# A linear-attention and GELU-MLP kernel: paired inverses on opposite corners, masked copies, casting and transposing DMAs

## Chip, cores and metric

The kernel runs on one core of a Trainium2 chip. The metric is the device time of one execution in microseconds. Lower is better.

## What is computed

The inputs are `q`, `k`, `v` (4 batches x 8 heads x 768 tokens x 48, float32), `beta` (4 x 8 x 768) and two MLP weights (384 x 2048 and 2048 x 384). First comes attention with a delta rule, token by token, and then an MLP over each token's 8 x 48 = 384 outputs:

```python
k_n = k / (np.linalg.norm(k, axis=-1, keepdims=True) + 1e-06)
for t in range(S):
    y[:, :, t] = einsum('bhd,bhde->bhe', q[:, :, t], state)
    v_old = einsum('bhde,bhd->bhe', state, k_n[:, :, t])
    state = state + beta[t] * einsum('bhd,bhe->bhde', k_n[:, :, t], v[:, :, t] - v_old)
...
out = gelu_tanh(x @ w_in) @ w_out
```

## The kernel before

**Chunks and units.** The 768 tokens are cut into 12 chunks of 64. The 32 pairs of batch and head are cut in two sets of 16. One chunk of one set is a *unit*: 24 units `u`, chunk `c = u // 2`. Within a unit, 16 small problems lie as 8 groups `g` by two partition halves `a` (partitions 0 to 63 and 64 to 127).

**One unit.** `prep(u)` normalizes `k` (POOL squares it, DVE sums, POOL takes the square root at L486, DVE adds and inverts), makes `kn`, `kb` (times beta) and `qb`, transposes them on TensorE (L506, 48 matmuls of 64x64) and copies the result to `kT` on DVE (L508). Two gram products follow (L529, L523); DVE multiplies them by masks into `mnd` (L532, L536), and POOL adds or subtracts an identity to make `lt` and `at` (L540, L542). The inverse of a 64x64 unit triangular matrix is then found by five Newton rounds (L558): `left` (L548) multiplies `lt` and `at` into a PSUM bank, DVE adds twice the identity and writes `qf`, `q4` or `q5` (L565), `right` (L553) multiplies that by `lt`, and ACT or DVE copies the result back to `lt` (L408 through L569). Each step needs the one before it.

`chain(u)` carries the state over chunks: `carried` (L589) and a subtraction (L605), `queries` (L594), `values` with the inverse (L599), the new state (L616, L622), the output `omat` (L627), and its copy to `xo`. When both units of a chunk are done, six DMAs on SP (L637) move 16 rows each of the fourth part of `xo` into the gaps of the other three, so that 384 features lie on 3 x 128 partitions.

**The MLP.** `mlp_up(c)` runs 16 blocks of `W1` (L651) with a GELU on ACT (L655); `mlp(u)` multiplies by `W2` (L668), copies to `ob` and stores. `weights()` loads both weights in float32 by DMAs on SP into two staging buffers `wst` (L452), and ACT and DVE cast them to bf16 (L408 through L457).

**Where matmuls lie in the array.** A small matmul uses one quarter of the array: input half by output half. Groups whose input and output halves are the same are mode `d` (diagonal), those that cross are mode `o`. Two groups, one of each mode, are issued interleaved by twos (`together`, L273) when the planner pairs them. The MLP, mode `m`, uses the whole array.

**The order.** Every operation is added to a list with its engines, a duration, a key and the buffers it reads and writes. `Flow.schedule` (L79) plays the list through, always taking the ready operation with the lowest key on each engine, and the order in which it places them becomes each engine's program. Where an operation names several engines, the planner chooses one. For TensorE it counts matmuls in blocks of 128 (`BLOCK`) and lets a block begin no sooner than 3.6 us after the last (`REFILL`). Key `2 * c + 4.5` places a chunk's MLP behind the units of some two chunks to come. `emit` turns dependencies into semaphore waits. Each engine then runs its list in order, and so does each DMA queue's issuer, SP, ACT or POOL.

Before the loop, DVE clears PSUM (L678) and POOL writes constant columns of `q4`, `q5`, `kn`, `kb` and `qb` (L681, L684).

Of the kernel before, what the change touches and what calls it, by code (L numbers as in the profile page):

```python
# [7 lines left out]
F32 = mybir.dt.float32  # L8
BF16 = mybir.dt.bfloat16
ALU = mybir.AluOpType  # L10
# [3 lines left out]
C = 64  # L14
# [9 lines left out]
class Flow:  # L24
# [6 lines left out]
    GROUP = {"d": 64, "o": 64, "x": 64}  # L31
    OTHER = {"d": "o", "o": "d"}
    SLACK = 0.6
    DMA_LAT = 2.2
    BLOCK = 128
    REFILL = 3.6
# [9 lines left out]
    def add(self, eng, fn, dur, reads=(), writes=(), key=0.0, alloc=(), accum=(), frees=(), mode=None, dma=None, n=16):  # L46
# [30 lines left out]
        return o  # L77

    def schedule(self):  # L79
# [78 lines left out]
        while done < len(self.ops):  # L158
            for e in ENGINES:
                while free[e] <= t + 1e-9:  # L160
# [6 lines left out]
                    if o.dma is not None:  # L167
                        dma_free = max(dma_free, t + 0.65) + d
                        free[e], o.t1 = t + 0.65, dma_free + self.DMA_LAT
                        self.queues[e].append(o)  # L170
                        heapq.heappush(events, (o.t1, o.seq, o))
                    elif e == "pe":
# [12 lines left out]
                        for k in range(first, many + 1, self.BLOCK):  # L185
                            at = start + extra + long * k / many
                            hold = max(0.0, self.begun + self.REFILL - at)
                            extra += hold
                            self.begun = at + hold
# [130 lines left out]
def bass_deltanet__then__act_gelu_tanh_kernel(  # L320
# [19 lines left out]
    with nc.allow_non_contiguous_dma("strided loads"), nc.allow_low_precision("bf16 pipeline"):  # L340
# [5 lines left out]
        NR, NP, NX = 3, 5, 3  # L346
        ident = sb("ident", [128, 128], F32)
        id64 = sb("id64", [128, C])
        two64 = sb("two64", [128, C])
        mfull = sb("mfull", [128, 2, 128], F32)  # L350
        mneg = sb("mneg", [128, C], F32)
        mup = sb("mup", [128, 2, C], F32)
        half = sb("half", [128, G], F32)
        braw = sb("braw", [32, NC, 2, C], F32)
        bsb = sb("bsb", [128, NC, 2 * G], F32)
# [3 lines left out]
        kn, kb, qb = (sb(n, [128, G, C], BF16, NP) for n in ("kn", "kb", "qb"))  # L359
        vb = sb("vb", [128, G, D], BF16, NP)  # L360
        kT = sb("kT", [128, 3, G, C], BF16, NP)
        mnd = sb("mnd", [128, 3, G, C], BF16, NP)
        at, lt, qf, q4, q5 = (sb(x, [128, G, C], BF16, NP) for x in ("at", "lt", "qf", "q4", "q5"))
        vd = sb("vd", [128, G, D], BF16, 3)
        us = sb("us", [128, G, D], BF16, 3)
        st = sb("st", [128, G, D], BF16, 4)
        xo = sb("xo", [128, J, 2, 128], BF16, NX)
        gT = sb("gT", [128, FC, 256], BF16, 2)
# [3 lines left out]
        wst = sb("wst", [128, FF], F32, 2)  # L372
# [5 lines left out]
        PEO, T1, T2 = 0.01, 0.0165, 0.029  # L378
        KUP, KSTEP, KDN = 4.5, 0.08, 0.6


        def const():
# [6 lines left out]
            for x, cm in ((0, 1), (1, -1)):  # L389
                A("pool", lambda e, P, x=x, cm=cm: e.affine_select(  # L390
                    out=mfull[:, x, :], in_=mfull[:, x, :], compare_op=ALU.is_gt, fill=0.0, base=0,
                    pattern=[[-cm, 128]], channel_multiplier=cm), 0.4, reads=["mfull"], writes=["mfull"])
            for a in range(2):
# [5 lines left out]
                A("dve", lambda e, P, r=r: e.tensor_copy(mneg[r, :], mfull[r, 0, r]), 0.25, reads=["mfull"], writes=[f"mneg{a}"])  # L399
                A("dve", lambda e, P, r=r: e.tensor_copy(mup[r, 0, :], mfull[r, 1, r]), 0.25, reads=["mfull"], writes=[f"mupa{a}"])  # L400
                A("dve", lambda e, P, r=r: e.tensor_scalar(mup[r, 1, :], mfull[r, 1, r], -1.0, None, op0=ALU.mult), 0.2,
                  reads=["mfull"], writes=[f"mupb{a}"])

        ID, TWO = ["id640", "id641"], ["two0", "two1"]
        MNEG, MUP = ["mneg0", "mneg1"], ["mupa0", "mupa1", "mupb0", "mupb1"]
# [7 lines left out]
        EV = ("act", "dve")  # L413

        def load_beta():
# [9 lines left out]
            for a in range(2):  # L425
                r = half_rows(a)
                A("dve", lambda e, P, a=a, r=r: e.tensor_copy(
                    bsb[r, :, :], P("psb")[r, 0:32 * NC].rearrange("p (c g a) -> p c g a", a=2, g=2 * G)[:, :, :, a]), 0.4,
                  writes=[f"bsb{a}"], frees=["psb"], key=-10)
        BS = ["bsb0", "bsb1"]  # L430

        def load(c):
            s = c % NR
            for n, src in (("k", k), ("q", q), ("v", v)):
                view = src.rearrange("b (j a) (c t) d -> a c t (b j) d", a=2, t=C)
                for bp in range(2) if c == 0 else (None,):
                    gs = slice(0, 2 * G) if bp is None else slice(G * bp, G * bp + G)
                    for a in range(2):
                        A(("sp", "act") if c == 0 else "sp", lambda e, P, n=n, a=a, view=view, gs=gs: e.dma_start(  # L439
                            raw[n][s][half_rows(a), gs, :], view[a, c, :, gs, :]),  # L440
                          1.2 if bp is None else 0.6, writes=[f"{n}raw{s}{x}" for x in ((0, 1) if bp is None else (bp,))],
                          dma=f"d{n}{s}" if bp is None else f"e{n}{bp}", key=2 * c - 4.0 + (bp or 0) - (2 if c < 2 else 0))

        def weights():
            wi = moe_w_in.rearrange("(h d) f -> h d f", d=D)
            idx = [0]

            def stage(parts, dst, cols, key, wname):
                i = idx[0] % 2
                idx[0] += 1  # L450
                for rows, src in parts:
                    A("sp", lambda e, P, i=i, rows=rows, src=src: e.dma_start(  # L452
                        wst[i][rows, 0:cols] if len(src.shape) == 2 else
                        wst[i][rows, 0:cols].rearrange("p (n e) -> p n e", e=DM), src),
                      4.5 / len(parts), writes=[f"wst{i}"], dma=f"w{i}", key=key)
                for c0 in range(0, cols, 512):
                    A(("act", "dve"), lambda e, P, i=i, c0=c0: copy(e, dst[:, c0:c0 + 512], wst[i][:, c0:c0 + 512]),  # L457
                      {"act": 0.62, "dve": 0.6}, reads=[f"wst{i}"], writes=[f"{wname}_{c0}"], key=key + 0.5)

            for t in range(3):  # L460
                parts = [(slice(0, 48), wi[2 * t]), (slice(48, 64), wi[6, 16 * t:16 * t + 16, :]),
                         (slice(64, 112), wi[2 * t + 1]), (slice(112, 128), wi[7, 16 * t:16 * t + 16, :])]
                stage(parts, W1[:, t, :], FF, -1.5 + 0.1 * t, f"W1{t}")
            w2v = moe_w_out.rearrange("(n p) e -> p n e", p=128)
            w2f = W2[:, :, :].rearrange("p n e -> p (n e)")
            for i in range(0, FC, 4):
                stage([(slice(0, 128), w2v[:, i:i + 4, :])], w2f[:, i * DM:(i + 4) * DM], 4 * DM, -1.2 + 0.02 * i, f"W2{i}")

        def prep(u):
# [9 lines left out]
            bcol = bsb[:, c, G * bp:G * bp + G].unsqueeze(2).to_broadcast(full)  # L479
            POOL = ("pool", "dve") if u < 2 else "pool"  # L480
            tt = {"pool": 0.84, "dve": 0.55}
            A(POOL, lambda e, P: e.tensor_tensor(sqs[:, :, :], kr, kr, ALU.mult), tt,  # L482
              reads=[f"kraw{r}"], writes=[sqn], key=u)
            A("dve", lambda e, P: e.tensor_reduce(nr[:, 0, :], sqs[:, :, :], AX.X, ALU.add), 0.55,  # L484
              reads=[sqn], writes=[n("nrm")], key=u)
            A("pool", lambda e, P: e.tensor_tensor(nr[:, 1, :], nr[:, 0, :], half[:, :], ALU.pow), 1.65,  # L486
              reads=[n("nrm"), "half"], writes=[n("nrm")], key=u)
            A("dve", lambda e, P: e.tensor_scalar(nr[:, 2, :], nr[:, 1, :], 1e-6, None, op0=ALU.add), 0.38,
              reads=[n("nrm")], writes=[n("nrm")], key=u)
            A("dve", lambda e, P: e.reciprocal(nr[:, 3, :], nr[:, 2, :]), 0.2, reads=[n("nrm")], writes=[n("nrm")], key=u)  # L490
            A(POOL, lambda e, P: e.tensor_tensor(kn[s][:, :, 0:D], kr,  # L491
                                                   nr[:, 3, :].unsqueeze(2).to_broadcast(full), ALU.mult), tt,
              reads=[f"kraw{r}", n("nrm")], writes=[n("kn")], key=u)
            A(POOL, lambda e, P: e.tensor_tensor(kb[s][:, :, 0:D], kn[s][:, :, 0:D], bcol, ALU.mult), tt,
              reads=[n("kn"), *BS], writes=[n("kb")], key=u)
            A(POOL, lambda e, P: e.tensor_copy(qb[s][:, :, 0:D], qr), {"pool": 0.5, "dve": 0.4}, reads=[f"qraw{r}"], writes=[n("qb")],
              key=u + 0.01)
# [228 lines left out]
```

## Time and profile before

| | |
|---|---|
| runs, us | 345.94, 345.88, 344.78 (median 345.88) |
| profiled execution, us | 342.66, its span 340.9 |
| busy: PE, DVE, ACT, POOL | 280.3, 216.6, 141.2, 186.1 us |
| matmuls | 8556, of which 960 are the MLP's |
| DMA | 27.04 MB in 84284 packets, 77552 of them under 512 B |
| MLP matmuls busy, L651 and L668 | 78.6 and 75.8 us |
| mean of one: L486, L540, L542 on POOL | 1651, 1162, 1153 ns |
| mean of one: L508, L532, L536 on DVE | 953, 684, 1217 ns |

PE is TensorE's matmuls, PEld its weight loads, SP the engine that issues most DMAs. The span runs from the first to the last instruction; the execution's time has a little more around it. In a view of instruction groups each line has the source line, the engine, the operation and the tiles (output, then inputs), the shapes and the count. "issue" as the cause of a wait means that the engine waited for nothing that the profile shows. Matmuls are pipelined, so that their busy times overlap and a busy PE is not one at its peak. The share of DMA is the mean over 16 DMA engines; in a stretch it can stand a little over 1.

### The profile page before, as it was taken

The numbers are of one execution on the slowest core, as the hardware profiler recorded it, in microseconds if no ns is written. First come the engines' busy times: TensorE is split into PE (matmuls) and PEld (weight loads), VectorE is DVE, ScalarE is ACT, GpSimd is POOL, SyncE is SP. The second block draws the span as 40 slices with busy tenths as digits, with TensorE's granted clock in tenths as the row PEclk, the third lists the DMA queues.
The fourth block names the chain that finished last, engine by engine and source line by source line (L and its number), as shares of the span: only waits on it lengthen the run. The fifth ranks groups of instructions, "written<-read, shape, count | busy, mean of one in ns | idle before, by whom it ended". The sixth has DMA issues, their size and how long they took to land.

```text
span 340.9 us, 18321 instructions
## 1 busy us (share of the span) xinstructions
PE 280.3 (82%) x8556; PEld 210.8 (62%) x8556; DVE 216.6 (64%) x383; ACT 141.2 (41%) x258; POOL 186.1 (55%) x222
## 2 busy tenths in 40 slices
PE   1354773596989997997998898899898999999994
PEld 1353763485766665775765667576666667676772
DVE  7686583575849887757876777767675485751100
ACT  1014212253455432553345444444455545455462
POOL 8995786288678988748637866735416132000000
PEclk9999999999999999999999999999999999999999
DMA  8999999869793256036025040020020010111121
GB/s 134 174 166 157 162 170 190 124 156 183 151 160 71 55 116 124 9 78 118 7 50 95 12 96 4 10 53 11 4 50 10 15 40 8 29 31 25 30 50 46
DMA packets 84284, 27.04 MB, mean 79 GB/s; under 512 B 77552, under 2 KB 83824, under 8 KB 83824
## 3 DMA queue, kind: packets, MB, share of 16 engines
q1 hardware_dynamic: 80512, 25.18, 41.4%
q8 instruction: 67, 1.10, 1.5%
q10 hardware_dynamic: 3696, 0.69, 1.4%
q14 instruction: 9, 0.07, 0.1%
HBM read 20.55 MB, written 4.72 MB: 74 GB/s over the span
## 4 chain that ended last, share of the span: by engine, by line
PE 74%; issue 9%; DVE 5%; SPq 5%; DMA 4%; ACT 2%
PE ps L651 21%; PE ps L668 20%; PE ps L553 9%; PE ps L548 8%; PE ps L506 5%; DMA wst<-in_moe_w_in_dram 4%; SPq L439 3%; PE ps L523 2%; PE ps L599 2%; PE ps L627 2%; PE ps L529 1%; PE ps L589 1%; SPq L452 1%; PE ps L594 1%; PE ps L616 1%
## 5 line engine op out<-in xcount | busy, mean ns | idle before, releaser
L655 ACT ACTIVATE gT<-ps 128x512 bf16<-128x512 f32 x96 | 57.3, 597 | 68.2 <-PE ps L651 67.2
L651 PE MATMUL ps<-xo,W 128*128 128x256 bf16 x576 | 78.6, 277 | 2.4 <-issue 1.8
L408 ACT ACTIVATE lt<-ps 128x512 bf16<-128x512 f32 (+2 forms) x88 | 46.6, 535 | 76.7 <-PE ps L553 68.9
L668 PE MATMUL ps<-W,gT 128*128 128x384 bf16 x384 | 75.8, 328 | 1.1 <-issue 1.0
L651 PEld LDWEIGHTS ps<-xo,W 128*128 128x128 bf16 x576 | 51.6, 99 | 14.3 <-issue 2.0
L548 PE MATMUL ps<-at,lt 64*64 64x64 bf16 (+2 forms) x1536 | 44.7, 198 | 3.7 <-DVE lt L408 1.2
L548 PEld LDWEIGHTS ps<-at,lt 64*64 64x64 bf16 x1536 | 35.6, 118 | 16.4 <-issue 8.5
L668 PEld LDWEIGHTS ps<-W,gT 128*128 128x128 bf16 x384 | 33.0, 98 | 18.9 <-issue 0.9
L553 PE MATMUL ps<-lt,qf 64*64 64x64 bf16 x1152 | 35.1, 204 | 11.0 <-issue 9.2
L542 POOL TENSOR_TENSOR at<-mnd,id 128x512 bf16<-128x512 bf16 x24 | 27.7, 1153 | 28.1 <-DVE mnd L532 27.0
L486 POOL TENSOR_TENSOR nrm<-nrm,half 128x8 f32<-128x8 f32 x24 | 39.6, 1651 | 4.9 <-DVE nrm L484 4.9
L565 DVE TENSOR_TENSOR qf<-ps,two 128x512 bf16<-128x512 f32 x48 | 32.7, 684 | 11.7 <-PE ps L589 6.5
L540 POOL TENSOR_TENSOR lt<-mnd,id 128x512 bf16<-128x512 bf16 x24 | 27.9, 1162 | 21.0 <-DVE mnd L536 19.9
L565 DVE TENSOR_TENSOR q<-ps,two 128x384 bf16<-128x384 f32 (+1 forms) x48 | 23.3, 487 | 24.8 <-PE ps L548 19.5
L553 PEld LDWEIGHTS ps<-lt,qf 64*64 64x64 bf16 x1152 | 27.2, 118 | 17.3 <-issue 10.8
L491 POOL TENSOR_TENSOR kn<-kraw,nrm 128x384 bf16<-128x384 f32 x24 | 19.9, 828 | 24.6 <-PE ps L627 16.7
L408 DVE CAST lt<-ps 128x512 bf16<-128x512 f32 (+2 forms) x32 | 19.2, 601 | 20.1 <-PE ps L553 13.8
L536 DVE TENSOR_TENSOR mnd<-ps,mup 128x1024 bf16<-128x1024 f32 x24 | 29.2, 1217 | 2.5 <-PE ps L523 2.3
L508 DVE COPY kT<-ps 112x1536 bf16<-112x1536 bf16 x24 | 22.8, 953 | 7.8 <-PE ps L506 7.3
L553 PE MATMUL ps<-lt,q 64*64 64x48 bf16 (+1 forms) x768 | 23.1, 193 | 5.3 <-issue 2.6
L553 PEld LDWEIGHTS ps<-lt,q 64*64 64x64 bf16 x768 | 17.8, 117 | 13.4 <-issue 6.9
L482 POOL TENSOR_TENSOR sq<-kraw 128x384 f32<-128x384 f32 x23 | 19.0, 827 | 5.4 <-DMA kraw<-in_k_dram 5.4
(72 smaller groups left out, 447.1 us busy)
## 6 DMA issues: line engine op xcount, KB each, us to landing
out_dram<-ob SPq DMA_DIRECT2D x48, 96.0 KB, 2.2
kraw<-in_k_dram SPq DMA_DIRECT2D x22, 192.0 KB, 5.2
qraw<-in_q_dram SPq DMA_DIRECT2D x22, 192.0 KB, 4.7
vraw<-in_v_dram SPq DMA_DIRECT2D x22, 192.0 KB, 5.5
wst<-in_moe_w_out_dram SPq DMA_DIRECT2D x4, 768.0 KB, 7.7
wst<-in_moe_w_in_dram SPq DMA_DIRECT2D x6, 384.0 KB, 7.5
xo<-xo SPq DMA_DIRECT2D x72, 8.0 KB, 2.2
wst<-in_moe_w_in_dram SPq DMA_DIRECT2D x6, 128.0 KB, 8.2
```

The source lines that it names most:

```text
L408: return e.activation(out, in_, ACT.Copy) if e is nc.scalar else e.tensor_copy(out, in_)
L486: A("pool", lambda e, P: e.tensor_tensor(nr[:, 1, :], nr[:, 0, :], half[:, :], ALU.pow), 1.65, reads=[n("nrm"), "half"], writes=[n("nrm")] ...
L508: A("dve", lambda e, P: e.tensor_copy(kT[s][0:DP, :, :, :].rearrange("p x g t -> p (x g t)"), P(ps("T")).bitcast(BF16)[0:DP, 0:3 * 512]), ...
L536: A("dve", lambda e, P: e.tensor_tensor(z0[:, 1:3, :, :].rearrange("p x g t -> p g x t"), P(ps("G")).rearrange("p (g x t) -> p g x t", x=2 ...
L540: A("pool", lambda e, P: e.tensor_tensor(lt[s][:, :, :], z0[:, 1, :, :], eye, ALU.add), 1.16, reads=[n("z0n")] + ID, writes=[n("lt")], key=u)
L542: A("pool", lambda e, P: e.tensor_tensor(at[s][:, :, :], z0[:, 0, :, :], eye, ALU.subtract), 1.16, reads=[n("z0m")] + ID, writes=[n("at")] ...
L548: yield e.matmul(cols(P, name, 0, g, w)[r, :], x[r, g, :], y[r, g, 0:w])
L553: yield e.matmul(cols(P, name, 0, g, C - lo, lo)[r, :], q[r, g, :], lt[s][r, g, lo:C])
L565: A("dve", lambda e, P, q=q, pq=pq, w=w, add=add: e.tensor_tensor(q[:, :, 0:w], g1(P, pq, 0, w), add[:, :, 0:w], ALU.add), 0.15 + 0.00104 ...
L651: yield e.matmul(P(ph)[:, 256 * f:256 * f + 256], W1[:, t, 128 * (i + f):128 * (i + f) + 128], xo[xi][:, t, :, :].rearrange("p b t -> p (b ...
L655: A("act", lambda e, P, i=i, ph=ph: e.activation(gT[gi][:, i:i + 2, :].rearrange("p f t -> p (f t)"), P(ph), ACT.Gelu_apprx_tanh), 0.62, f ...
L668: yield e.matmul(P(po)[:, 0:DM], g_[:, f, 128 * bp:128 * bp + 128], W2[:, f, :], start=(f == 0), stop=(f == FC - 1))
```

## The change

The planner gets a mode `z`, a longer `DMA_LAT` (2.6), 4.0 for weights, 1.5 us for a DMA issue on POOL and `SLOWFILL`: 5.5 us per block of 128 matmuls before 45 us. A chunk's MLP key falls to `2.5 + 0.75 * c` for the first chunks. `NP`, the number of unit buffers, goes from 5 to 6, and `prep`'s keys are 2 lower.

*Two inverses in step.* `newton(us)` takes both units of a chunk, the second one phase behind (chunk 0's two units stay apart). `right` writes to the opposite half in rounds 1 to 4 (mode `o`), so `lt` changes halves every round; `at` therefore holds both halves. One unit's `left` and the other's `right` are one operation of 32 matmuls. Round 4's `right` covers 64 columns instead of 48.

*Masked copies.* `lt` and `at` start as stored identities, written in the first pass for all six buffers; `copy_predicated` puts the masked gram over them from PSUM. The second gram product is made twice (32 matmuls), for both halves. `beta` is also kept negated, so the carried term is added.

*Four corners.* `kqb` holds two heads side by side in its 128 columns, so a transposed head lies in either half. Grams, `carried`, `queries` and the new state then take the corners of the array in turn and write two PSUM banks.

*Transposes.* Units 0 to 7: 12 matmuls of 128x128 on TensorE, copied by ACT or DVE. Units 8 to 23: one DMA transpose each on SP.

*Weights.* Six DMAs on POOL's queue cast float32 to bf16 on the way: two halves of `W1` behind the first `kn`, four quarters of `W2` behind the third. The staging and its casts are gone. The loads of chunks 2 and 3 wait for the second and third `kn`.

*x.* Ten DMAs a chunk (48 rows, or 32 and 16) put each head's rows in their place in a new tile `xn`, where there were six of 16 rows.

*Start.* DVE and ACT clear half of PSUM each. ACT takes the squares and the casts of `q` for units up to 7 where the planner chooses so, and the square root for units 0 to 3.

```diff
-    DMA_LAT = 2.2
+    DMA_LAT, WLAT, SOFT = 2.6, 4.0, 1.5
-    REFILL = 3.6
+    REFILL, SLOWFILL, SLOWTIL = 3.6, 5.5, 45.0
...
+        for x in range(2):
+            cs = slice(FF // 2 * x, FF // 2 * x + FF // 2)
+            held.setdefault(W1AT[x], []).append(A("pool", lambda e, P, cs=cs: e.dma_start(W1[:, :, cs], w1v[:, :, cs]), W1DUR,
+                                                  writes=[f"W1{x}"], dma=f"w1{x}", key=W1AT[x] + WKEY))
...
+            if u < UT:
+                        yield e.transpose(t[:, 128 * i:128 * i + 128], kqb[s][:, i // J, 2 * (i % J):2 * (i % J) + 2, :].rearrange("p b d -> p (b d)"),
+                                          idb[:, :])
+            else:
+                A("sp", lambda e, P: e.dma_start_transpose(kT[s][:, :, :], kqb[s][:, :, :, :].rearrange("p x g d -> p (x g d)")), 1.6,
+                  reads=[n("kn"), n("kb"), n("qb")], writes=[n("kT")], dma=f"t{s}", key=u)
...
-            A("pool", lambda e, P: e.tensor_tensor(lt[s][:, :, :], z0[:, 1, :, :], eye, ALU.add), 1.16,
-            A("pool", lambda e, P: e.tensor_tensor(at[s][:, :, :], z0[:, 0, :, :], eye, ALU.subtract), 1.16,
+            A("dve", lambda e, P: e.copy_predicated(
+                at[s].rearrange("p x (y h) t -> p y x (h t)", y=2), wide(mlow),
+                P(ps("G2")).rearrange("p (y x m) -> p y x m", y=2, x=2)), 1.22,
+            A("dve", lambda e, P: e.copy_predicated(lt[s][:, :, :], mupp[:, 0, :].unsqueeze(1).to_broadcast([128, G, C]), g4(P, 0)), 0.69,
...
+        def both(f, g):
+            def run(e, P):
+                x, y = f(e, P), g(e, P)
+                left = [x, x, y, y] * G
+                yield from (i for z in left if (i := next(z, None)) is not None)
...
+        def newton(us):
+            for phase in range(10 + len(us) - 1):
+                parts = [(u, step(u, phase - k)) for k, u in enumerate(us) if 0 <= phase - k < 10]
+                if len(parts) == 2 and parts[0][1][3] != parts[1][1][3]:
+                    (u, x), (_, y) = parts
+                    A("pe", both(x[0], y[0]), TZ + PEO + (0.24 if us[0] < UQ else 0), n=34 if us[0] < UQ else 32, reads=x[1] + y[1], alloc=[(x[2], 1), (y[2], 1)], mode="z", key=u)
...
+            if u < 2 * CZ:
+                newton([u])
+            elif u % 2:
+                newton([u - 1, u])
```

In the changed kernel's lines, L544 and L536 are the two grams, L578 and L592 `left` and `right`, L585 the addition on DVE, L636 `carried`, L641 `queries`, L664 the new state, L678 the output, L708 and L725 the MLP's matmuls.

## The prediction

> **What bounds the kernel now.** I read the page, then a table by stage, then TensorE's waits, then its timeline, then the DMA queues. The kernel has two stages, split by the first MLP matmul, which the timeline has at 86.89 us.
>
> ```profile
> span 340.9 us, 18321 instructions
> 0.00:86.90 86.90, 47.92 (x1693) 43.26 (x1693) 58.02 (x107) 22.60 (x42) 65.79 (x97) 1.00 1.01 163
> 86.90:340.90 254.00, 232.33 (x6868) 167.58 (x6864) 158.56 (x277) 118.58 (x217) 120.30 (x125) 1.00 0.25 51
> ```
>
> Columns: stretch, length, busy time of PE, PEld, DVE, ACT, POOL, granted clock, DMA share, GB/s. In the first 86.9 us TensorE is busy for 48 us and the 16 DMA engines all the time (share 1.01, 163 GB/s). In the other 254.0 us TensorE is busy for 91% and the DMA engines for a quarter: there TensorE is the bound.
>
> ```profile
> 50.33 0.44 PE L599 MATMUL ps<-vb,lt 64*64 64x48 bf16 x10
> 55.42 0.90 PE L553 MATMUL ps<-lt,qf 64*64 64x64 bf16 x26 [4.65 <-issue]
> 86.89 2.74 PE L651 MATMUL ps<-xo,W 128*128 128x256 bf16 x12
> ...
> 231.37 0.44 PE L553 MATMUL ps<-lt,qf 64*64 64x64 bf16 x16
> ...
> 233.28 0.19 PE L548 MATMUL ps<-at,lt 64*64 64x48 bf16 x2
> 233.29 0.21 PE L589 MATMUL ps<-st,kT 48*64 48x48 bf16 x2
> 233.31 0.19 PE L548 MATMUL ps<-at,lt 64*64 64x48 bf16 x2
> ...
> 234.63 0.83 PE L651 MATMUL ps<-xo,W 128*128 128x256 bf16 x6
> 235.30 0.81 PE L668 MATMUL ps<-W,gT 128*128 128x384 bf16 x4
> ```
>
> Three prices come from these rows, as (row's time less one matmul's own) over the steps in it. Sixteen 64-wide matmuls alone: (0.44-0.20)/15 = 16 ns each. Two groups on opposite corners, interleaved by twos: four matmuls in 0.03 us (233.28 to 233.31); the median over all such stretches is 8.5 ns a matmul. MLP: (0.83-0.27)/5 = 0.11 us at L651, (0.81-0.33)/3 = 0.16 us at L668; start to start the records have 0.109 and 0.163. At 86.89 the same L651 takes (2.74-0.42)/11 = 0.21 us: until about 90 us matmuls run at half this pace, although the table grants clock 1.00 throughout.
>
> ```profile
> q8 instruction: 67, 1.10, 1.5%
> PE ps L553 <- issue: 4.8, 9, 1.0
> PE ps L506 <- issue: 3.5, 4, 1.3
> PE ps L548 <- DVE mnd L536: 0.3, 1, 0.3
> ```
>
> The first line is a DMA queue, the others TensorE's waits after 87 us (total, times, longest). 67 packets of 16 KB for 8556 matmuls are 128 matmuls a packet, and these waits come every 128th matmul: TensorE waits for its own instructions, hardly for another engine. Packets start 3.5 us apart at the least; while the DMA engines are full, 8.0 us (44.4 to 52.4 us, the 4.65 us stall above).
> [...]
>
> **The change, second stage.** I sum the 254.0 us first. MLP: 576 x 0.109 + 384 x 0.163 = 125.4. Small matmuls after the first MLP, counted in the program's order: 2738 in groups of their own x 16 ns = 43.8; 3166 interleaved x 8.5 ns = 26.9, with 2.2 for the 272 that are 128 wide. Switches between MLP and small: 118 times there and back, 0.142 and 0.23 us start to start, less the streaming in them, 0.22 a pair, = 26. Feed stalls and waits over 0.3 us: 19. That is 243.3; 10.7 remain (gaps between groups, the last store after 336 us).
> After the change, in its program order: the MLP is the same, 125.4. Newton's 160 matmuls a unit stay 160, but one unit's `left` (diagonal) now interleaves with the other's `right` (off-diagonal). Alone stand 1218 x 16 ns = 19.5; interleaved 2270 x 8.5 = 19.3; 1408 go over all four corners (L544, L636, L641, L664) x 8.5 = 12.0, and 256 of L536, 128 wide, x 16.5 = 4.2. The corner groups have no row of their own: bounds are 8.5 ns (interleaved row) and 16 ns (a group alone), 10.6 us apart; the order of corners is that of the interleaved row, so 8.5. No transposes are left there (PE ones end with unit 7). Switches: 98 x 0.22 = 21.6. Feed: (7884-1772)/128 = 47.8 blocks against 53.6, stalls 19 x 47.8/53.6 = 17. With the 10.7 kept: 229.7, a gain of 24.3 us.
>
> Off TensorE in that stage: DVE loses the `kT` copy (953 ns x 24) and the half of L536 that made `lt`'s input; it gains copy_predicated. That operation has no row. L536, the same PSUM source, 1024 elements a partition, takes 1.22 us, L532 with 512 0.68; the other end is twice that, if it reads its destination too. I take 1.22 + 0.68, as the elements are the same; the dear end is 24 x 1.9 = 46 us of DVE. With 72 x 0.68 (L585) and the rest counted alike DVE has 223 us against 216.6, some 168 of them in this stage of 230: 73%, hidden behind TensorE. POOL loses `at` and `lt` (24 x 2.3 = 55 us) and some squares and casts: 186 to about 113. ACT gains 7 `kT` copies and 26 more `lt` copies: 141 to about 160. Both stay below TensorE, and fewer POOL steps shorten each unit's way: a gain only where TensorE waits for it, which the waits price at under 1 us.
>
> SP: x goes from 72 to 120 issues of 0.59 us (median at L637), 10 a chunk in place of 6, so a chunk's x is 2.4 us later. What hides it is the MLP work in stock: in 320 to 340.9 us TensorE has MLP alone. Without that cover it would cost 12 x 2.4 = 29 us. Sixteen DMA transposes of 0.39 MB join SP's queue, each waiting for POOL's `kqb`, with later loads, x and stores behind it. [...] Their landing, taken as a load's here (median 5.0 us at L439), is covered by six unit buffers; uncovered it would cost a unit those 5 us.
>
> **First stage.** Three resources give three sums. DMA: the first MLP needs x of chunk 0, which in SP's new order stands behind 5.3 chunks of k, q, v (1.18 MB each, 6.3 MB), and W1 (3.1 MB): 9.4 MB / 163 GB/s = 58 us; with W2's 3.1 MB taking its share, 77. Before, x of chunk 0 was issued at 63.9 us behind 10.6 MB, the same rate. Feed: 1772 matmuls stand before the first MLP, against 1692; 12 packets after the one at about 20 us, at 3.5 to 5.4 us (the mean before, (86.9-21.6)/12): 62 to 85. DVE: its list up to there sums to 55 us against 58.0, as the weights' casts (part of 11 x 0.6) and `kT` go and the identities' fills come; at 67% busy as now, 82; at 85%, 65. What goes is the waiting: both POOL steps of 1.15 us between gram and Newton, ACT's and DVE's casts of W1, the square root on POOL (1.65 us), and SP's eight W1 issues. The six weight DMAs move to POOL, behind the first `kn` and the third; they pass SP's whole queue, and POOL's `sq`, `vb` and `kn` wait behind their issue. That issue has no row; between 0.42 and 9.2 us (SP's shortest and longest), I take 1 us, under 6 in all, on a POOL that saves 12 us in this stage. Whether a casting DMA moves bytes more slowly no row tells: W1's plain packets take 17 us of all engines now (384 x 726 ns / 16); twice that at the dear end would land W1 at about 50 us, still ahead of x. I take 72 us, between the lowest and highest sums, range 60 to 86.
> [...]
>
> **Sum.** 72 + 229.7 = 301.7 us of span, 303.5 with the 1.8 between span and profiled time (342.66). The median of the runs, 345.88, is 1.0094 times that: 306.
>
> **Rivals.**
> The start does not shrink: DMA and feed keep it at 87 us, since nearly the same bytes and 80 more matmuls stand before the first MLP. 87 + 230 gives 322. For it speaks share 1.01; against it, of the 31 us of TensorE's gaps over 0.3 us from 13 to 87 us only some 17 lie at a packet's edge; the rest are waits for work that the change shortens.
> The start falls to the lowest sums: 58 us by DMA, W2 late, and fewer feed stalls, 225 after it: 288. Against it: the feed's 62.
> DVE becomes the bound: copy_predicated at twice its rows makes 269 us of DVE, 203 in the second stage, 88%. Rounds then wait for DVE; if a third of the 35 extra us shows, 12 later, and 5 in the start: 323. For it: no row shows the operation.
> SP becomes the bound, the other side: the transposes hold SP's queue. [...] Against it: 0.25 DMA share and loads of the same size issued in under 1 us at the median.
>
> **How the numbers follow.** Forecast 0.45; start as before 0.20; start at its lowest 0.17; DVE 0.08; SP 0.10. The forecast's own range is 60 to 86 us for the start with 222 to 238 after it, 286 to 329; with the rivals it is 280 to 332. A difference under 0.5% can't be told from none here. Faster: all but SP and a sliver, 0.88; same 0.02; slower 0.10.
>
> **What would show it.** First MLP matmul at 60 to 86 us; TensorE over 85% busy after it; 62 instruction packets; corner groups with four matmuls in 0.03 us; copy_predicated rows near 1.2 and 0.7 us; transposes under 6.5 us on SP. A first MLP after 87 us, DVE over 85%, or SP waits ahead of x would make it wrong.

## The result and the profile after

The changed kernel takes 332.85 us (331.25 to 333.95, 4 runs) against 345.33 before on the same chip: ratio 0.964, 95% interval 0.959 to 0.969. Measured twice more beside other experiments, unchanged, it had 0.983 (0.972 to 0.994) and 0.976 (0.971 to 0.982); so below, differences of less than about 2% between chips, or 1% on one chip, are not read. The sign was right and the size was not: 306 was predicted, with 280 to 332 as range. Executions that ran some per cent longer than the fastest of their kernel (e5's profiled one at 464 us among them) are left out of the ratios, and as the profiles of e1, e4, f2 and h1 are of such executions, mainly places in the order, start times, falls of the clock and causes of waits are taken from them.

The page and the table by stage of the kernel after (stretch, length, busy PE, PEld, DVE, ACT, POOL, granted clock, DMA share, GB/s); the profiled execution took 333.95 us:

```profile
span 331.9 us, 17015 instructions
PE 264.9 (80%) x7884; PEld 194.7 (59%) x7884; DVE 210.1 (63%) x383; ACT 158.9 (48%) x282; POOL 123.8 (37%) x151
PEclk9999555555589999986997999999999999999989
q8 instruction: 62, 1.02, 1.3%
```

```profile
0.00:89.80 89.80, 51.58 (x1773) 43.84 (x1773) 66.84 (x127) 40.02 (x66) 45.47 (x64) 0.68 0.92 144
89.80:331.90 242.10, 213.36 (x6115) 150.87 (x6112) 143.27 (x257) 118.91 (x216) 78.31 (x88) 0.97 0.44 78
```

The stage up to the first MLP matmul is 2.9 us longer than before (86.9), not shorter by 15. The rest fell from 254.0 to 242.1 us, about half of the predicted fall. POOL gave up 62 us; the span fell by 9. TensorE is busy for 88% of the second stage against 91%.

TensorE's waits in the same kernel (total, times, longest), two lines out of the list of all, and two groups on DVE:

```profile
PE ps L708 <- DMA xn<-xo: 8.9, 4, 3.0
PE ps L592 <- issue: 8.0, 6, 3.3
```

```profile
L548 DVE CAST_PREDICATED at<-mlow,ps 128x1024 bf16<-128x1024 uint16 x24 | 29.2, 1217 | 2.0 <-PE ps L544 1.9
L553 DVE CAST_PREDICATED lt<-mupp,ps 128x512 bf16<-128x512 uint16 x24 | 16.3, 681 | 0.0
```

The first line is new: the MLP waits for x. The two on DVE are priced as forecast (1.22 and 0.68 us). What one such wait for x does, from the timeline (start, length, what, idle before):

```profile
148.78 1.46 PE L708 MATMUL ps<-xn,W 128*128 128x256 bf16 x6 [2.19 <-DMA xn<-xo]
...
151.14 1.46 PE L708 MATMUL ps<-xn,W 128*128 128x256 bf16 x6
...
153.50 1.29 PE L708 MATMUL ps<-xn,W 128*128 128x256 bf16 x6
...
155.46 0.82 PE L725 MATMUL ps<-W,gT 128*128 128x384 bf16 x4
```

Six such matmuls take 0.83 us at full clock (at 173.63 us of the same timeline); here 1.46. The four stretches around them:

```profile
144.23:147.65 3.42, 1.68 (x108) 1.20 (x96) 3.42 (x7) 1.36 (x3) 0.00 (x0) 1.00 0.14 34
147.65:151.06 3.41, 2.28 (x38) 1.63 (x38) 0.55 (x1) 0.78 (x2) 0.00 (x0) 0.50 0.50 114
151.06:154.47 3.41, 3.41 (x49) 2.44 (x46) 2.48 (x5) 1.20 (x3) 0.00 (x0) 0.50 0.89 170
154.47:157.89 3.42, 3.42 (x157) 2.39 (x155) 2.21 (x6) 1.54 (x3) 1.98 (x3) 1.00 0.55 79
```

Here a stretch in which TensorE was busy for 1.68 of 3.42 us is followed by 6.8 us at half clock, and the wholly busy one at the end of those by full clock. So this wait is paid twice: in itself, and in the slower matmuls beside it. Of the four waits for x, which end at 148.8, 173.6, 241.5 and 315.5 us, three have half clock beside them (records from 147.7, 175.0 and 314.9 us); the one of 1.25 us before 241.5 has none.

For the comparison of all kernels I split TensorE's time by the gaps from one matmul's start to the next: small to small, MLP to MLP, between the two kinds, and every gap over 0.3 us (whole) as a wait; behind an MLP matmul the bound is 0.36 us, since at half clock the matmul behind one of L708 starts as much as 0.351 us after it with no wait (three times in after, 149.8 to 175.7 us). Each row is one profiled execution; the second profile of after (f1) has 32.1 us of waits in the second stage beside 30.2, so differences of a few us in that column mean little. In us:

| kernel | first MLP at (after n matmuls) | waits before it | small | MLP | switches | waits | ratio to before |
|---|---|---|---|---|---|---|---|
| before | 86.9 (1692) | 40.8 | 73.7 | 111.5 | 42.2 | 21.9 | 1 |
| after | 89.8 (1772) | 38.8 | 54.4 | 118.0 | 34.7 | 30.2 | 0.964, 0.983, 0.976 |
| e2, two queues | 91.1 (1740) | 42.2 | 56.2 | 115.4 | 37.4 | 25.6 | 0.975 |
| e3, no step | 87.3 (1996) | 32.3 | 61.1 | 113.8 | 38.0 | 20.7 | 0.967 |
| f4, late, two queues | 86.8 (1740) | 37.6 | 54.9 | 114.8 | 33.5 | 28.9 | 0.965 |
| f3, no step, two queues | 89.9 (1948) | 32.6 | 60.3 | 113.0 | 40.4 | 17.7 | 0.964 |
| g3, no step, late, two queues | 89.9 (1948) | 32.8 | 61.0 | 113.2 | 39.0 | 14.1 | 0.949 |

(The columns from "small" on are of the second stage.) From before to after the small matmuls gave 19.3 us and the switches 7.5; the MLP took back 6.5 and the waits 8.3. The first stage is made of the time up to TensorE's first matmul (5.4 us before, 8.1 after), the waits, and the rest, which is matmuls at their pace (40.7 and 42.8 us). So 2.7 of its 2.9 us more lie ahead of the first matmul; of the other two, one is 2.0 us less and the other 2.1 more.

### The profile page after: what moved, and what is told of

It reads as the page before. It is cut to its first block, busy times and chain, and to the rows that moved or that the text cites. A ratio compares the mean times of both kernels' runs of the same rounds, so it can differ in the third digit from the quotient of the medians.

```text
span 331.9 us, 17015 instructions
## 1 busy us (share of the span) xinstructions
PE 264.9 (80%) x7884; PEld 194.7 (59%) x7884; DVE 210.1 (63%) x383; ACT 158.9 (48%) x282; POOL 123.8 (37%) x151
## 3 DMA queue, kind: packets, MB, share of 16 engines
q0 software_dynamic: 2912, 3.15, 5.8%
## 4 chain that ended last, share of the span: by engine, by line
PE 56%; DVE 13%; SPq 9%; issue 8%; POOL 5%; DMA 5%; ACT 2%
PE ps L708 19%; PE ps L725 13%; SPq L692 9%; PE ps L592 6%; PE ps L578 6%; DMA xn<-xo 3%; PE ps L520 3%; DVE at L548 2%; PE ps L649 2%; DVE qf L585 2%; PE ps L678 2%; DMA kT<-kqb 2%; POOL kqb L509 1%; POOL kqb L506 1%; PE ps L544 1%
## 5 line engine op out<-in xcount | busy, mean ns | idle before, releaser
L708 PE MATMUL ps<-xn,W 128*128 128x256 bf16 x576 | 81.8, 287 | 10.1 <-DMA xn<-xo 8.9
L424 ACT ACTIVATE lt<-ps 128x512 bf16<-128x512 f32 (+1 forms) x94 | 52.4, 560 | 62.6 <-PE ps L592 36.9
L725 PE MATMUL ps<-W,gT 128*128 128x384 bf16 x384 | 74.3, 327 | 0.0
L578 PE MATMUL ps<-at,lt 64*64 64x64 bf16 (+2 forms) x1920 | 59.0, 203 | 13.6 <-issue 5.8
L708 PEld LDWEIGHTS ps<-xn,W 128*128 128x128 bf16 x576 | 54.3, 102 | 23.0 <-DMA xn<-xo 8.5
L578 PEld LDWEIGHTS ps<-at,lt 64*64 64x64 bf16 x1920 | 46.3, 120 | 28.3 <-issue 13.6
L585 DVE TENSOR_TENSOR qf<-ps,two 128x512 bf16<-128x512 f32 x72 | 48.9, 684 | 16.5 <-PE ps L592 7.5
L501 POOL TENSOR_TENSOR nrm<-nrm,half 128x8 f32<-128x8 f32 x20 | 32.8, 1640 | 42.6 <-DVE nrm L495 41.8
L725 PEld LDWEIGHTS ps<-W,gT 128*128 128x128 bf16 x384 | 33.8, 98 | 18.5 <-DVE xo L424 0.2
L592 PE MATMUL ps<-lt,qf 64*64 64x64 bf16 x1152 | 37.2, 206 | 8.8 <-issue 7.5
L585 DVE TENSOR_TENSOR q<-ps,two 128x384 bf16<-128x384 f32 (+1 forms) x48 | 23.4, 487 | 21.2 <-PE ps L578 12.3
L592 PEld LDWEIGHTS ps<-lt,qf 64*64 64x64 bf16 x1152 | 28.2, 118 | 10.9 <-issue 7.3
L506 POOL TENSOR_TENSOR kqb<-kraw,nrm 128x384 bf16<-128x384 f32 x23 | 19.1, 830 | 40.6 <-PE ps L664 34.4
L548 DVE CAST_PREDICATED at<-mlow,ps 128x1024 bf16<-128x1024 uint16 x24 | 29.2, 1217 | 2.0 <-PE ps L544 1.9
L592 PE MATMUL ps<-lt,q 64*64 64x64 bf16 (+1 forms) x768 | 23.2, 199 | 2.2 <-ACT lt L424 1.5
L424 DVE CAST lt<-ps 128x512 bf16<-128x512 f32 (+1 forms) x26 | 15.6, 606 | 13.8 <-PE ps L578 8.2
L592 PEld LDWEIGHTS ps<-lt,q 64*64 64x64 bf16 x768 | 18.4, 121 | 7.1 <-issue 3.8
L513 POOL TENSOR_TENSOR vb<-vraw,bsb 128x384 bf16<-128x384 f32 x24 | 19.8, 830 | 2.2 <-DVE vd L655 2.2
L509 POOL TENSOR_TENSOR kqb<-kqb,bsb 128x384 bf16<-128x384 bf16 x22 | 18.3, 830 | 0.7
```

The source lines that it names most:

```text
L424: return e.activation(out, in_, ACT.Copy) if e is nc.scalar else e.tensor_copy(out, in_)
L506: A(POOL, lambda e, P: e.tensor_tensor(kq(0), split(kr), split(nr[:, 3, :].unsqueeze(2).to_broadcast(full)), ALU.mult), tt, reads=[f"kraw{ ...
L509: A(POOL, lambda e, P: e.tensor_tensor(kq(1), kq(0), split(bneg), ALU.mult), tt, reads=[n("kn"), *BN], writes=[n("kb")], key=u - PK)
L548: A("dve", lambda e, P: e.copy_predicated(at[s].rearrange("p x (y h) t -> p y x (h t)", y=2), wide(mlow), P(ps("G2")).rearrange("p (y x m) ...
L578: yield e.matmul(P(pq)[r, C * g:C * g + w], lt[s][r, g, :], at[s][r, f, g, 0:w], start=u >= UQ, stop=True, skip_group_check=True)
L585: A("dve", lambda e, P: e.tensor_tensor(q[:, :, 0:w], bank(P, pq, 0, w), two64[:, 0:w].unsqueeze(1).to_broadcast([128, G, w]), ALU.add), 0 ...
```

## The experiments

All edits are to the kernel after.

**e1: x priced as landing soon, so the MLP is ordered early.**

```diff
+                        if o.dma[0] == "x":
+                            o.t1 = t + issue + self.DMA_LAT
```

> One change to the kernel after: the planner lets a transfer of x arrive at its issue + 2.6 us, instead of behind the queued bytes of the weights, so TensorE's written order has the first MLP matmul after 996 matmuls in place of 1772. Theory A (the order holds the first MLP back; in the kernel after, x of chunk 0 was issued by 62.8 us and the weights had landed by 40, yet the first MLP matmul came at 89.8 us): first MLP matmul at 65 to 72 us, TensorE busy for more of the first 90 us than 51.6 us, time 8 to 15 us less than 332.9. Rival B (instruction feed, VectorE or the half clock set the pace of the first 90 us whatever the order): first MLP matmul earlier, but the time within 3 us of 332.9, because the small matmuls that were moved back are missing as cover or cost the same later.

The first MLP matmul came at 64.4 us, after 996 matmuls, but the ratio is 0.990 (0.978 to 1.001): no gain. A is right about the order and wrong about the time; B holds. The clock rose at 68.5 us, 24 us earlier than in after, and fell to half again four times by 191 us (for 3.4, 10, 7 and 17 us). The likely reading is that the MLP had been the work that filled the later holes.

**e2: five of a chunk's ten x issues on ScalarE.**

```diff
-                        A("sp", lambda e, P, h=h, lo=lo, hi=hi: e.dma_start(
+                        A("act" if h % 2 else "sp", lambda e, P, h=h, lo=lo, hi=hi: e.dma_start(
```

(The two halves also get a semaphore each.)

> One change to the kernel after: of the ten x transfers of a chunk, those of the odd heads (five) are issued by ScalarE, the others by SP. Theory C (ten issues of 0.6 us one behind the other on SP delay x, and TensorE waits 8.9 us for it in the second stage, with half clock behind each wait): the wait of L708 on the DMA of xn falls from 8.9 us to under 4, time 4 to 8 us less than 332.9. Rival D (the wait is set by when the chain delivers xo, not by the issues; ScalarE's 60 issues of 0.6 us push its copies back): wait as before, time 0 to 6 us more.

The wait for xn fell to 2.8 us as C had it; the time shows no gain: 332.3 us, 0.975 (0.969 to 0.981), among the three ratios of after. By the table the waits of the second stage fell by 4.6 us, and those of the first grew by 3.4, foremost `PE ps L520 <- POOL kqb L509` with 8.1 us (2.3 in after).

**e3: no inverses in step.**

```diff
-        CZ, TZ, LAT = 1, 0.296, {2: 1, 3: 2}
+        CZ, TZ, LAT = NC, 0.296, {2: 1, 3: 2}
```

> One change to the kernel after, taken back: every chunk's two inverses run on their own (as units 0 and 1 do) and are interleaved only where the planner finds a partner. In its order 1184 more matmuls after the first MLP stand alone on one diagonal (2400 against 1216), and 10 more switches there and back. Theory E (alone 16 ns, interleaved 8.5 ns): 1184 x 7.5 ns = 9 us and 2 us of switches, time 5 to 12 us more than 332.9 (some of it may be in the first stage: 1996 matmuls stand before the first MLP, against 1772). Rival F (TensorE's waits, not its streaming, set the second stage, and two inverses in step wait on each other's copies): time within 3 us of 332.9.

330.4 us, 0.967 (0.960 to 0.975): F, though not for lack of streaming. By the table the step's streaming is there (54.4 us against 61.1, with 224 more matmuls in the stage), and there are 3.3 us less of switches; both are paid back in waits (30.2 against 20.7, and 38.8 against 32.3 in the first stage) and in the MLP (118.0 against 113.8). The wait on xn is gone too.

**e4: all transposes on TensorE** (`UT` from 8 to 24).

> One change to the kernel after, taken back in part: all 24 units are transposed by TensorE (12 of 128x128, with a copy of 1.0 to 1.5 us on ScalarE or VectorE), none by a DMA. Theory G (the DMA transposes are worth having): 16 units x (0.7 us of TensorE, plus a packet of instructions for 192 matmuls, plus switches) = 12 to 16 us more TensorE, less what SP's freed 32 us take off the waits for x (8.9 us): time 4 to 12 us more than 332.9. Rival H (SP's transposes, in order ahead of x and of loads, cost more than they save): time 0 to 8 us less.

345.8 us, 1.009 (1.003 to 1.016): G, at the upper end or above. The 288 transposes are busy for 26.0 us on its page, where after's 96 are for 11.9; at 57 ns each, as at full clock in e8 below, the 192 more stream for 11 us, an estimate. By the three ratios of after the DMA transposes are worth 2.6 to 4.5%, as much as the whole change (1.7 to 3.6%).

**e5 and f1: the kernel after again.**

> The kernel after, unchanged, beside the next three on one chip: the earlier runs stood on a chip whose median of before was 341.0 us, the first measurement of after on one with 345.3. Expected ratio to before 0.96 to 0.975. Its clock should again stand at 0.5 from about 31 to about 90 us, and fall for single 3.41 us stretches after waits.

> The kernel after, unchanged, as the measure for the next three on their chip. Expected 332 to 336 us, 0.965 to 0.985 of before.

0.983, above what was expected of e5, and 0.976. The profile of e5 has no clock record. In f1's profile the clock fell again after waits (three stretches after 92 us and one at the end), and xn was waited for 6.4 us.

**e6: weights staged in float32 and cast**, much as before (`wst`, seven transfers on SP, 24 casts on ScalarE and VectorE, 12 each, in place of the six casting DMAs).

> One change to the kernel after, taken back: the weights come through two f32 staging tiles by SP (7 transfers) and are cast by 28 copies of 0.6 us on ScalarE and VectorE, as in the kernel before; no casting DMAs on POOL. Theory I (casting DMAs shorten the start: SP and the casts' time come free): time 3 to 10 us more than after. Rival J (the first stage is set by TensorE's order and half clock, with weights landed by 40 us in after, far ahead of the first MLP at 89.8): time within 3 us of after; the first MLP in its order stands after 1532 matmuls, 240 earlier, so the first MLP matmul comes at 80 to 90 us.

1.012 (1.005 to 1.019) beside 0.983 for after on that chip: I, about 10 us. J is right about the place (82.4 us, after 1532 matmuls) and wrong about the time: the second stage has 42.4 us of waits.

**e7: masks multiplied, identities added on POOL.** The products go to two new tiles, and POOL works on them:

```diff
-            A("dve", lambda e, P: e.copy_predicated(lt[s][:, :, :], mupp[:, 0, :].unsqueeze(1).to_broadcast([128, G, C]), g4(P, 0)), 0.69,
+            A("dve", lambda e, P: e.tensor_tensor(zl[s][:, :, :], g4(P, 0), mcau[:, :].unsqueeze(1).to_broadcast([128, G, C]), ALU.mult), 0.69,
...
+            A("pool", lambda e, P: e.tensor_tensor(lt[s][:, :, :], zl[s][:, :, :], id64[:, :].unsqueeze(1).to_broadcast([128, G, C]), ALU.add), 1.16,
```

> One change to the kernel after, taken back: the grams are multiplied by masks on VectorE (same sizes), and POOL adds or subtracts the identity (1024 and 512 elements a partition, some 2.3 and 1.2 us a unit); no copy_predicated, no stored identities. Theory K (as predicted: POOL's two steps are hidden behind TensorE, under 1 us in the second stage; in the first stage they lengthen each unit's way): time 0 to 4 us more than after. Rival L (the shorter way from gram to inverse is what made the kernel faster): 6 us or more above after.

0.993 (0.988 to 0.999) beside 0.983 (0.972 to 0.994): about 3.6 us, the upper end of K, and not told apart from nothing on that chip. The waits of the first stage grow to 48.9 us. Of POOL's 74 us more, 21 fall in the first stage and 53 beside TensorE in the second. TensorE's first matmul comes at 5.5 us, as in the kernel before, where after and the other runs that store the identities have 8.1: so filling them is the likely reason for the later start.

**e8: matmuls as filler.**

```diff
+            def warm(e, P, i):
+                for _ in range(1):
+                    yield e.matmul(P(f"F{i}.{u}")[:, 0:512].rearrange("p (x t) -> p x t", x=4), idb[:, :], idb[:, :].unsqueeze(1).to_broadcast([128, 4, 128]))
```

> One addition to the kernel after: 80 matmuls of 128x128x512 on the identity (10 after each of the first eight units' transposes, results never read), which the planner puts where it sees TensorE idle ahead of the first MLP; nothing else. [...] Rival V (the clock only follows; feed and waits set the first stage): full clock or not, first MLP at 90 us or later, time 0 to 8 us more.

The fillers were to raise the clock of the first stage, and it did rise. The clock row of e8, and the twelve transposes of one unit in the timelines of after, then of e8:

```profile
PEclk9999975999899987979999999999999999999878
```

```profile
53.27 1.46 PE L520 MATMUL ps<-idb,kqb 128*128 128x128 bf16 x12 [0.90 <-POOL kqb L509]
```

```profile
58.30 0.84 PE L520 MATMUL ps<-idb,kqb 128*128 128x128 bf16 x12
```

Between 31 and 85 us after stands at half clock all along; e8 for 17 us in all. Yet the first MLP came at 91.2 us, and the ratio is 0.984 beside 0.983: V by both numbers. From one start to the next the fillers take 24.9 us of the stage. The other matmuls, 96 more than in after, stream for 35.7 us (42.8) and wait for 22.5 (38.8). So the higher clock did shorten them, and nothing came of it; how much the fillers themselves stood in the way of work that was ready, this run does not show.

**f2, f3, f4: a later MLP, and pairs of edits.** f2 adds 1.0 to `KUP`; f3 is e3 and e2 together, f4 is f2 and e2.

```diff
-        KUP = [min(4.5, 2.5 + 0.75 * c) for c in range(NC)]
+        KUP = [min(4.5, 2.5 + 0.75 * c) + 1.0 for c in range(NC)]
```

> One change to the kernel after: the MLP of every chunk gets a planner key 1.0 higher, so it is due half a chunk later; the in-step inverses stay. Theory M (in step, both units of a chunk deliver their output together and late, so x reaches TensorE just when the MLP is due; a later due time hides it): the waits of L708 on xn fall from 8.9 us to under 3 and the single half-clock stretches behind them go, time 5 to 9 us less than after. Rival N (the MLP moved back leaves holes elsewhere, as where it was moved forward in the first experiment): waits over 0.3 us in the second stage stay at 30 us or more, time within 3 us of after.

> Two edits to the kernel after together: no inverses in step, and x issued by SP and ScalarE by halves. Without the step the waits on xn had gone already (largest under 2 us in all), so the second queue has little left to take: time within 2 us of the run without the step (330.4). If the issues themselves cost (10 in a row on SP), 3 to 5 us less than that.

> Two edits to the kernel after together: MLP due later by 1.0, and x by two queues. By theory M waits on xn all but gone (under 1 us), time 6 to 11 us less than after. By rival N no less than after minus 3 us.

0.967 (0.960 to 0.974), 0.964 (0.957 to 0.971) and 0.965 (0.959 to 0.971), beside 0.976 (0.971 to 0.982): each some 1% better than after, the least that is read here. The waits for xn are 1.3 us in f2 and none in f3 and f4; the gain is 3 to 4 us where M had 5 to 9 for f2 and 6 to 11 for f4. For f4 that is unsure: its six times run from 325.7 to 338.7 us, and its two lowest would put it some 7 us under after. f3 is where e3 was (0.964 and 0.967). f4 keeps 28.9 us of waits with none of them on xn, so the lateness of x explains only part of what the step costs.

**g1: four of ten phases in the inverses of the first eight units** (their inverse is left unfinished, so the kernel leaves work out).

```diff
-            for phase in range(10 + len(us) - 1):
+            last = 4 if us[0] < 8 else 10
+            for phase in range(last + len(us) - 1):
```

> One change to the kernel after, which leaves work out: the inverses of the first eight units (chunks 0 to 3) run 4 of their 10 phases, 768 matmuls fewer and 48 copies fewer (36.8 us of VectorE and ScalarE at most); these units' results are then another matrix. Theory P (TensorE with its packets, 128 matmuls in 5.1 us each from 23.8 to 90.3 us in after, and the inverse's round trips set the first stage): 6 packets fewer, time 22 to 31 us less than after, first MLP before 80 us. Rival Q (loads, norms and POOL's preparation of units set it): time 4 to 14 us less, first MLP at 82 us or later.

324.3 us, 0.948 (0.942 to 0.954), first MLP at 82.4: Q by both numbers. 768 matmuls fewer take 9.0 us of streaming from the first stage (42.8 to 33.8) and 4.8 from the second; the time falls by 6 to 12 us, by the lowest and highest ratio of after. The waits of the first stage stay, at 40.3 us, but their causes change: from 12 us to the first MLP the profile puts 1.4 us of them down to issue (10.4 in after) and 31.0 to other engines (19.6). With fewer instructions to feed, TensorE waits for the units' preparation instead.

**g2: roots of units 4 to 7 on ScalarE** (`US` from 4 to 8).

> One change to the kernel after: the square roots of units 4 to 7 are taken by ScalarE (0.25 us) as those of units 0 to 3 are, not by POOL's power (1.6 us). By Q above: four steps of 1.4 us out of the chain of waits, first MLP 2 to 5 us earlier, time 2 to 5 us less than after. By P: within 2 us of after.

0.989 (0.980 to 0.999), first MLP at 91.6 us: not Q, and beside 0.964 to 0.983 for after on other chips no gain. Taking the roots from POOL does not shorten the stage; whether the kernel became slower can't be said across chips, and the order changed with it (1900 matmuls before the first MLP, 1772 in after).

**g3 and g4: three edits together, and g2's on top.**

> Three edits to the kernel after together: no inverses in step, MLP due later by 1.0, x by two queues. If all three work on one cause (waits for x, 8.9 us), this is no better than any two of them: 328 to 332 us. If they are several causes: under 327 us.

> The three edits of the run before, and ScalarE's roots for units 4 to 7. By Q 2 to 5 us less than that run, by P the same within 2 us.

g3 is the fastest: 324.75 us, 0.949 (0.944 to 0.954), below 327, as several causes would have it. The pairs stood on another chip, and 1.5% below the best of them is within what is not read between chips, so that is not settled. g4, on g3's chip, is at 0.979 (0.973 to 0.986), clearly slower; why is open. g3's span and chain of waits by engine, after's chain being `PE 56%; DVE 13%; SPq 9%; issue 8%; POOL 5%; DMA 5%; ACT 2%`:

```profile
span 322.2 us, 16961 instructions
...
PE 71%; DVE 9%; issue 6%; ACTq 5%; ACT 5%; POOL 2%
```

TensorE has 15 points more of the chain, DMA has gone from it, and DMA issues (SPq and ACTq) fell from 9% to 5%.

**h1 and h2: the weights' transfers priced at what they took**, in after and in g3.

```diff
-        KSTEP, KDN, W1DUR, W2DUR = 0.08, 0.6, 8.5, 4.2
+        KSTEP, KDN, W1DUR, W2DUR = 0.08, 0.6, 4.8, 2.4
```

> One change to the kernel after: the planner prices the weights' transfers at 4.8 and 2.4 us in place of 8.5 and 4.2 (the trace of after gives all six 5.8% of 16 engines' 331.9 us, that is 19.3 us). Nothing but the order of the engines' work follows from it; the first MLP stands after 1612 matmuls, not 1772. Theory R (the order keeps the preparation of units 4 to 7 behind work that it need not wait for): the square of unit 4 starts before 38 us (42.3 in after), POOL's longest wait in the first stage falls from 13.3 us to under 9, first MLP at 78 to 84 us, time 5 to 12 us less than after. Rival S (as with x alone in the first experiment, an earlier order only moves the holes): first MLP earlier, time within 3 us of after.

> The same price in the fastest version so far (no inverses in step, MLP due later, x by two queues; 324.75 us, 0.949 of before). By R 5 to 10 us less, 315 to 320 us; by S 322 to 328 us.

POOL's waits in the first 90 us of after, which called for it:

```profile
POOL nrm L501 <- DVE nrm L495: 34.4, 4, 13.3
```

In h1 unit 4's square starts at 32.4 us (42.3), POOL's longest wait is 4.5 us, and the first MLP comes at 79.8, all as R has it; the ratio is 0.972 (0.965 to 0.980), that of after: S. h2 has 0.963 (0.955 to 0.971): no gain over g3's 0.949 on another chip, and neither R nor S.

## Why the prediction missed

*Prices.* Most held. Small matmuls: predicted 72.9 to 55.0 us in the second stage, measured 73.7 to 54.4. The four-corner groups (L544, L636, L641, L664) start a matmul every 7.3 to 8.3 ns in the mean where the clock is full (8.5 taken), so they do run at the interleaved pace. Switches gave 7.5 us (4.4 predicted). 62 packets, as counted. Masked copies 1217 and 681 ns. DMA transposes held SP for 2.02 us at the median and landed 5.2 us after issue (5 taken). No run shows the 6.5 us that the forecast's last line allows them as a limit; the longest of the sixteen held SP for 4.01 us. A casting DMA held POOL for 0.75 to 1.0 us (1 taken), and the weights had landed by 40 us. VectorE was busy for 210 us, so the rival with VectorE as the bound is out, and so is SP as the bound: the sixteen transposes held it for 34.5 us in all.

*The first stage: 72 us taken, 89.8 measured* (17.8 of the 30.2 us that the span was off). The step that failed is "What goes is the waiting". The steps that it names did go, and the waits stayed: 40.8 us before, 38.8 after. TensorE's waits from 12 us to the first MLP: the two largest of the kernel before, then the two largest of after for another engine; and the longest piece of the chain that ended last in the kernel before (start, length):

```profile
PE ps L553 <- issue: 7.0, 4, 4.7
PE ps L506 <- DVE kb L494: 6.2, 1, 6.2
PE ps L520 <- DVE kqb L509: 4.5, 1, 4.5
PE ps L520 <- POOL kqb L509: 2.3, 2, 1.4
```

```profile
17.76 12.98 DMA wst<-in_moe_w_in_dram
```

Summed over all lines of that view, waits put down to issue fell from 15.3 to 10.4 us, and those for other engines, which the change was to shorten, went from 18.0 to 19.6. The rest of the stage is 8.1 us before the first matmul and 42.8 us of matmuls, at half clock from 31.6 us on by the records, for which none of the three sums had a term.

The rival "the start does not shrink" came true in its number, but not for its reason. By DMA the sum was right (x of chunk 0 was issued by 62.8 us), and between 12 us and the first MLP after's chain holds no transfer, where the kernel before had the 13 us of `wst` shown. The feed alone does not hold it either: g1 took nearly all issue waits away, and others took their place. None of the other candidates is the limit by itself: the MLP's place (e1), the clock (e8), POOL's roots (g2) and earlier preparation (h1) were changed, and the time did not fall. Each of these runs changed the order too, and matmuls left out (g1) gave no more than their own streaming, and nothing for the packets saved. Most likely several limits lie close together; what would shorten the 38.8 us of waits stays open. Without the step they are 32 to 33. Also wrong was the measure itself: where the first MLP stands is a choice of the order, and in e1, e6 and h1 it came 7 to 25 us earlier with no gain in time.

*The second stage: 229.7 us summed, 242.1 measured.* Even with the rival's 87 us for the start, 322 us, some 11 us would be missing; they are here. Against the sum's terms the small matmuls gave 1.4 us more and the switches 3.1; the waits, summed at 2 us less, came out 8.3 more, and the MLP, summed as unchanged, 6.5 more. The two that were better hid part of the two that failed.

"What hides it is the MLP work in stock" failed, and 8.9 us of waits for x showed; e2, f2 and f4 take most or all of these away. From the end of a chunk's last x issue to its first MLP matmul there are 3.2 us (median of the fourth to the eleventh chunk; 1.2 to 4.9), and 10.5 before (6.5 to 17.7). The 2.4 us of issues are the smaller part of that loss: without the step (e3), with the same ten issues on SP, it is 8.1 us, and TensorE doesn't wait for x. In step the later of a chunk's two outputs is copied to `xo` 10.4 to 13.6 us ahead of the chunk's MLP, in e3 14.2 to 17.6. So the step delivers late, as M had it.

And the sum had TensorE at full clock, with no term for what follows a wait: 16.9 us of the stage are at half clock. Before it was 3.6, up to the first clock record and judged by the pace of the matmuls. Half the difference is 6.6 us, an estimate, where the MLP grew by 6.5.

The third piece, found with e3, f3 and g3, is that the step itself brings waits: where it is undone they fall by 8 to 15 us (30.2 to 20.7, 25.6 to 17.7, 28.9 to 14.1 in the three pairs of the table). That is about what it saves there in streaming (4 to 7 us) and switches (3 to 5.5) together, and the MLP is 1.6 to 4.2 us longer with it; the stages also differ by some 200 matmuls. The spans of the profiled executions are 1.6 to 6.3 us shorter without it, all one way (331.9 to 325.6, 330.6 to 326.2, 323.8 to 322.2), but each pair stood on two chips and is within 2%. I had priced a pair of inverses by its matmuls alone. That each phase must now wait for two copies instead of one is the likely reason; no run shows it by itself.

*What the gain came from.* Taken back one at a time, the DMA transposes cost 2.6 to 4.5%, the casting DMAs 3%, the masked copies about 1%, which is not told from nothing, and the step nothing that shows. These do not add up to the whole; each edit also reorders the rest.

## What to carry to other kernels

Price a matmul group with its wait and with the clock that follows the wait (16.9 us at half clock in after's second stage, 3.6 in before's), not by its streaming alone: interleaving two dependent chains saved streaming and switches here, 7.1 to 11.6 us in the three pairs, and lost about as much again in waits, 8 to 15. In a kernel ordered by hand or planner, the start of a stage is a place in the order and not a cost; undo one part at a time and compare whole times. Watch how far a new transfer's landing is from its first use, since a hidden one becomes a wait with a small shift: here x had 3.2 us from its last issue to its first use, 10.5 before, and 8.9 us of waits for it showed.

## What the hardware showed

*The clock.* In after and before each clock record but the last covers a multiple of 3.41 us, at 1.0 or at 0.5. I set the share of each such 3.41 us in which any matmul ran against the clock of the next, all but the last record. In after 66 were at full clock: the four that half clock followed were busy for 0.31 to 0.49, the other 62 for 0.59 or more. In before there were 72, busy for 0.60 or more, and none was followed by half clock. Of after's 22 at half clock, four were followed by full clock, busy for 0.82, 1.00, 1.00 and 1.00; the other 18 were busy for 0.40 to 0.83. Two traces make no rule of this: between 0.49 and 0.59 they have no stretch at full clock, and at half clock 0.82 went both ways (314.9 and 76.0 us).

*Before the first clock record the page shows full clock, and it need not be.* The transposes tell. In after, whose first record begins at 28.2 us, those at 14.1, 18.1 and 24.3 us start 104 ns apart, where the page's row has 9s; so do those at 35.5 and 53.3 us, which are recorded at half clock. The twelve of e8 at 58.30 us, shown above, start 57 ns apart: 0.84 us less one's own 0.21, over 11.

*Casting DMAs are cheap in bytes.* The six read 6.3 MB of float32 and count as 3.15 MB and 5.8% of 16 engines, 19.3 us, landing 7.9 to 13.5 us after issue.
